# A decode block on one core: norm 2 folded around w_in, the weight loads reordered, and one V tile loaded in 112 + 8 + 8 rows

## The chip, the cores and the metric

The kernel runs on one core of one Trainium2 chip. The metric is the device time of one execution in microseconds (us); the times given are medians of repeated runs.

## The reference, cut to what matters

An adaptive-norm block for four tokens (B = 4, one position each): cached attention with 32 heads of 128 over 4096 keys, then a gated MLP ("gMLP"). The two caches, 4 x 32 x 4096 x 128 in bf16 each, are 268 MB of the 283 MB that are read.

```python
mod = (_silu(c) @ w_mod).reshape(c.shape[0], 6, 1, -1)
sa, ca, ga, sb, cb, gb = (mod[:, 0].copy(), ..., mod[:, 5].copy())
h = _layernorm(x, axis=-1) * (1 + ca) + sa
x = x + ga * _A_ref(h, A_k_cache, A_v_cache, A_wq, A_wo)
h = _layernorm(x, axis=-1) * (1 + cb) + sb
x = x + gb * _B_ref(h, B_w_in, B_w_sp, B_b_sp, B_w_out)
```

`_A_ref` is softmax attention of one query per head over the cache, then the product with `wo` (4096 x 512). `_B_ref` is `z = gelu(h @ w_in)` (512 x 1792), split in two halves of 896; the second half is layer-normed, scaled by `w_sp` and shifted by `b_sp` (one number each here, since there is one position), and multiplied with the first; then the product with `w_out` (896 x 512).

## The kernel before, in words

**Tiles.** The work on the caches is cut into 32 "quads" (`quads`, four heads of one token each): group g = 0 to 7 of heads outside, token b = 0 to 3 inside. For a quad, 4 heads x 4096 keys are laid on 128 partitions, 32 per head, so that each partition holds 128 keys of 128 elements: a K tile and a V tile of 128 x 16384 bf16 each, 4 MB, with one contiguous row of 32 KB per partition. `load` (L83) allocates a tile from two buffers and issues its loads on the SP queue. `load_v` (L95) and `load_k` (L92) load every tile with one DMA, except the last, which comes in column parts (V: a half, a quarter, two eighths), so that its work can begin with the first part.

**Order.** The program is scheduled by hand; each engine works its instructions in the order in which they stand. All loads that matter are on the SP queue[...]: `wm01` (the columns of w_mod for norm 1), `wq0`, K(0), K(1), wo of group 0, V(0), the rest of wq, and then in turn i: K(i+1), for b = 0 the tile `wo_g` of the group (512 KB, L368, read with 1 KB per partition and head), V(i). In turn 8 the columns 2 to 5 of w_mod follow (`wm25`, L382, 2 MB). After the last V come w_in (L409) and w_out (L411), into one tile.

**A turn i** of the loop at L362: `diagonal(i-2)`, the first half of `scores(i)` (DVE multiplies K with the query in place, L251; PE sums over the head dimension with the identity, L256), `project(i-2)`, the second half of the scores, `values(i-1)`, then `fold` and `softmax` of quad i. `values` (L299) multiplies the V tile with P on PE in four row groups (L309) and lets ACT drain the result (L315); ACT makes P with four Exp instructions (L286). `diagonal` (L322) picks the right block out of it. `zsum` (L295) gives the sum of P into one half of the PSUM tile `zo_ps`, whose other half takes the output. `project` takes the reciprocal (L344), scales (L345) and, for b = 3, adds the product with the group's wo to `attn_ps` (L352).

**The end.** The last quad takes another way: `values_last` (L333) multiplies block after block of V as weights with four columns of P, as the parts of V land, with filler matmuls (`keep_busy`, L127) between. Then x1 = x + ga * attn (L414, L415); the statistics of norm 2 (`ln_stats`, L147 to L165: square on DVE, one matmul with a constant, a reduction, Ln and Exp on ACT); the normed and modulated h2T (L420 to L424); 56 matmuls with w_in (L431); gelu (L438, L442); the statistics of norm 3; 28 matmuls with w_out (L449); the gate, scale and shift (L454 to L468); a transpose (L470) and the store. `mod_part` (L190) computes one of the six parts of `mod` with 16 matmuls; in turn 10 it is called for parts 2 to 5, with `wm25`.

Of the kernel before, what the change touches and what calls it, by code (L numbers as in the profile page):

```python
# [8 lines left out]
BF16 = mybir.dt.bfloat16  # L9
F32 = mybir.dt.float32  # L10
# [6 lines left out]
def kernel(  # L17
# [16 lines left out]
    nc = tc.nc  # L34
# [48 lines left out]
    def load(cache, i, tag, parts):  # L83
        t = kvp.tile([P, NT * DH], BF16, name=tag, bufs=2)
        a = 0
        for part in parts:
            b = a + NT * DH // part
            nc.sync.dma_start(out=t[:, a:b], in_=kv_view(cache, i)[:, a:b])
            a = b
        return t.rearrange("p (n d) -> p n d", d=DH)  # L90
# [2 lines left out]
        return load(A_k_cache, i, "kt", (2, 2) if i == len(quads) - 1 else (1,))  # L93

    def load_v(i):  # L95
        return load(A_v_cache, i, "vt", (2, 4, 8, 8) if i == len(quads) - 1 else (1,))

    NQ = len(quads)

# [22 lines left out]
    def keep_busy(n):  # L122

        if busy_ps[0] is None:
            busy_ps[0] = psum_s.tile([P, 4 * P], F32, name="big", bufs=2)
        for _ in range(n):
            nc.tensor.matmul(busy_ps[0], lhsT=ident, rhs=wide, start=True, stop=True)  # L127
# [14 lines left out]
    def bc(col, n):  # L142
        return col[:, None, :].to_broadcast([P, n, B])
# [24 lines left out]

    modT = persist.tile([P, 6, J, B], F32, name="modT")
    qbc = persist.tile([P, B, G, DH], BF16, name="qbc")  # L170
    x1b = persist.tile([P, 2, J, B], F32, name="x1b")
    wbf = persist.tile([P, 2], F32, name="wbf")
    xcT = persist.tile([P, J, 2 * B], F32, name="xcT")
# [8 lines left out]
        tc.tile_pool(name="psum_s", bufs=1, space=bass.MemoryType.PSUM)  # L182
    )

    def mod_part(wt, w0, oc):
        ps = psum_s.tile([P, J, B], F32, name="small", bufs=1)
        for jo in range(J):
            for j in range(J):
                c0 = (oc - w0) * D + jo * P
                nc.tensor.matmul(  # L190
                    ps[:, jo, :], lhsT=wt[:, j, c0:c0 + P],
                    rhs=sT[:, j, :], start=(j == 0), stop=(j == J - 1),
                )
        if oc in (1, 4):
            nc.vector.tensor_scalar_add(out=modT[:, oc], in0=ps, scalar1=1.0)
        else:
            nc.vector.tensor_copy(out=modT[:, oc], in_=ps)
# [46 lines left out]
    with tc.tile_pool(name="psum_att", bufs=1, space=bass.MemoryType.PSUM) as psum:  # L244
# [47 lines left out]
        def zsum(i):  # L292
            zo = psum.tile([P, 2, NH], F32, name="zo_ps", bufs=2)
            st["z", i], st["o", i] = zo[:, 0], zo[:, 1]
            nc.tensor.matmul(  # L295
                st["z", i], lhsT=ones_f, rhs=rs4s[i % NB], start=True, stop=True,
            )
# [29 lines left out]
        def values_last(i):  # L327
            P4 = P4s[i % NB]
            zsum(i)
            for n in range(NT):  # L330
                if n in (NT // 2, 3 * NT // 4, 7 * NT // 8):
                    keep_busy(2)
                nc.tensor.matmul(  # L333
                    st["o", i], lhsT=st["v", i][:, n, :], rhs=P4[:, n, :],
                    start=(n == 0), stop=(n == NT - 1),
                )

        def project(i):
            g, b = quads[i]
            if b == 0:  # L340
                st["oT", g] = wk.tile([P, NH, B], BF16, name="oT", bufs=2)
            oT = st["oT", g]
            rz = wk.tile([P, NH], F32, name="rz", bufs=2)
            nc.vector.reciprocal(out=rz, in_=st.pop(("z", i)))  # L344
            nc.vector.tensor_tensor(  # L345
                out=oT[:, :, b], in0=st.pop(("o", i)), in1=rz, op=ALU.mult,
            )
            if b == B - 1:
                wo_g = st.pop(("wo", g))
                for hl in range(NH):  # L350
                    for jo in range(J):
                        nc.tensor.matmul(  # L352
                            attn_ps[:, jo, :], lhsT=wo_g[:, hl, jo * P:(jo + 1) * P], rhs=oT[:, hl, :],
                            start=(g == 0 and hl == 0 and jo == 0),
                            stop=(g == G - 1 and hl == NH - 1),
                            skip_group_check=True,
                        )

        wo_v = A_wo.rearrange("(h p) n -> p h n", p=P)
        st["k", 0] = load_k(0)  # L360
        for i in range(NQ + 1):
            if i + 1 < NQ:  # L362
                st["k", i + 1] = load_k(i + 1)
            if i < NQ:
                if quads[i][1] == 0:
                    g = quads[i][0]
                    t = wk.tile([P, NH, D], BF16, name="wo_g", bufs=2)
                    nc.sync.dma_start(out=t, in_=wo_v[:, g * NH:(g + 1) * NH, :])  # L368
                    st["wo", g] = t
                st["v", i] = load_v(i)  # L370
                if i == 0:
                    wq_r = kvp.tile([P, J, (G - 1) * GW], BF16, name="wt", bufs=1)
                    nc.sync.dma_start(out=wq_r, in_=wq_v[:, :, GW:])
                if i in (2, 3):
                    for b in (2 * i - 4, 2 * i - 3):
                        for g0, n in ((1, 3), (4, 4)):
                            qp = psum_s.tile([P, n, DH], F32, name="big", bufs=2)
                            query(wq_r, 1, b, g0, n, qp, 0)
                            nc.scalar.copy(out=qbc[:, b, g0:g0 + n, :], in_=qp)  # L379
                if i == 8:  # L380
                    wm25 = kvp.tile([P, J, 4 * D], BF16, name="wt", bufs=1)
                    nc.sync.dma_start(out=wm25, in_=wmod_v[:, :, 2 * D:])  # L382
                if i == 10:
                    for oc in range(2, 6):
                        mod_part(wm25, 2, oc)
            if i > 1:
                diagonal(i - 2)
            if i < NQ:
                scores(i, 0)
            if i > 1:  # L390
                project(i - 2)
            if i < NQ:
                scores(i, 1)
            if 0 < i < NQ:
                values(i - 1)
            if i < NQ:
                fold(i, 0)
                fold(i, 1)
                softmax(i)
        keep_busy(3)  # L400
        values_last(NQ - 1)
        project(NQ - 1)
# [1 line left out]

    with tc.tile_pool(name="post", bufs=1) as post, \
            tc.tile_pool(name="psum_post", bufs=1, space=bass.MemoryType.PSUM) as psum:
        wt = kvp.tile([P, J * F + JF * D], BF16, name="wt", bufs=1)
        win = wt[:, 0:J * F].rearrange("p (j n) -> p j n", j=J)
        nc.sync.dma_start(out=win, in_=B_w_in.rearrange("(j p) n -> p j n", p=P))  # L409
        wout = wt[:, J * F:].rearrange("p (j n) -> p j n", j=JF)  # L410
        nc.sync.dma_start(out=wout, in_=B_w_out.rearrange("(p j) n -> p j n", j=JF))  # L411

        x1 = x1b[:, 0]
        nc.vector.tensor_tensor(out=x1, in0=attn_ps, in1=modT[:, 2], op=ALU.mult)  # L414
        nc.vector.tensor_tensor(out=x1, in0=x1, in1=xT, op=ALU.add)  # L415
        mean, rstd = ln_stats(post, psum_s, x1b, mean_d, J, "ln2")
        nc.scalar.preload_act_table_set("gelu_apprx_tanh_and_others")
        keep_busy(5)
        h2 = post.tile([P, J, B], F32, name="h2")
        nc.vector.tensor_tensor(out=h2, in0=x1, in1=bc(mean, J), op=ALU.subtract)  # L420
        nc.vector.tensor_tensor(out=h2, in0=h2, in1=bc(rstd, J), op=ALU.mult)
        nc.vector.tensor_tensor(out=h2, in0=h2, in1=modT[:, 4], op=ALU.mult)
        h2T = post.tile([P, J, B], BF16, name="h2T")
        nc.vector.tensor_tensor(out=h2T, in0=h2, in1=modT[:, 3], op=ALU.add)  # L424


        z_ps = psum.tile([P, 2, JF, B], F32, name="zf_ps")
        for s in (1, 0):
            for jf in range(JF):
                for j in range(J):  # L430
                    nc.tensor.matmul(  # L431
                        z_ps[:, s, jf, :], lhsT=win[:, j, s * FH + jf:(s + 1) * FH:JF],
                        rhs=h2T[:, j, :], start=(j == 0), stop=(j == J - 1),
                    )
        keep_busy(1)
        z2b = post.tile([P, 2, JF, B], F32, name="z2b")
        z2 = z2b[:, 0]
        nc.scalar.activation(out=z2, in_=z_ps[:, 1], func=AF.Gelu_apprx_tanh)  # L438


        u = post.tile([P, JF, 2, B], BF16, name="u")
        nc.scalar.activation(out=u[:, :, 1, :], in_=z_ps[:, 0], func=AF.Gelu_apprx_tanh)  # L442
        nc.scalar.preload_act_table_set("natural_log_exp_and_others")
        mean, rstd = ln_stats(post, psum_s, z2b, mean_f, JF, "ln3", lambda:
            nc.vector.tensor_tensor(out=u[:, :, 0, :], in0=u[:, :, 1, :], in1=z2, op=ALU.mult))
# [20 lines left out]
        )  # L466
        yo = post.tile([P, B, J], BF16, name="yo")
        nc.vector.tensor_tensor(out=yo.rearrange("p b j -> p j b"), in0=q, in1=r1, op=ALU.add)  # L468
        t_ps = psum.tile([J * B, P], F32, name="t_ps")
        nc.tensor.matmul(  # L470
            t_ps, lhsT=yo.rearrange("p b j -> p (b j)"), rhs=ident, start=True, stop=True,
        )
# [33 lines left out]
```

## Time and profile before

| | us |
|---|---|
| median of 10 runs (676.89 to 677.72) | 677.36 |
| the profiled execution | 677.3 |
| its span, first to last instruction | 675.4 |
| PE busy / DVE busy / ACT busy in the span | 419.6 / 375.8 / 102.9 |
| bytes read from HBM, mean rate | 282.73 MB, 419 GB/s |

The profile is one execution. "PEld" is the weight load of PE, which overlaps its matmuls. In the timeline a line gives start, duration, engine, line and operation, output and inputs with the shape, how many, and in brackets the idle time before and what ended it. DMA queues are named by number: q1 is that of SP, q8 and q14 carry instructions to the engines. The trace also has each DMA packet's start, duration and size, and for every DMA the times at which the DMA engines that take part report completion; it doesn't name the engine of a packet.

### The profile page before, as it was taken

The numbers are of one execution on the slowest core, as the hardware profiler recorded it, in microseconds if no ns is written. First come the engines' busy times: TensorE is split into PE (matmuls) and PEld (weight loads), VectorE is DVE, ScalarE is ACT, GpSimd is POOL, SyncE is SP. The second block draws the span as 40 slices with busy tenths as digits, with TensorE's granted clock in tenths as the row PEclk, the third lists the DMA queues.
The fourth block names the chain that finished last, engine by engine and source line by source line (L and its number), as shares of the span: only waits on it lengthen the run. The fifth ranks groups of instructions, "written<-read, shape, count | busy, mean of one in ns | idle before, by whom it ended". The sixth has DMA issues, their size and how long they took to land.

```text
span 675.4 us, 6968 instructions
## 1 busy us (share of the span) xinstructions
PE 419.6 (62%) x2979; PEld 205.5 (30%) x2983; DVE 375.8 (56%) x401; ACT 102.9 (15%) x311; POOL 4.1 (1%) x18
## 2 busy tenths in 40 slices
PE   2574857755657664567656457765555765565786
PEld 2232423322224222233223223332222322222344
DVE  2665555566653565545656455566654565664732
ACT  1021211101111011111011111101111101111112
POOL 2000000000000000000000000000000000000000
PEclk9977888766778676788667788766778876677885
DMA  9999999999999999999999999999999999999993
GB/s 373 414 423 434 430 434 422 428 429 432 435 428 416 433 430 433 426 431 428 431 428 427 432 435 422 426 431 433 430 429 420 434 433 433 432 419 432 426 413 127
DMA packets 16942, 283.17 MB, mean 419 GB/s; under 512 B 1416, under 2 KB 6032, under 8 KB 8464
## 3 DMA queue, kind: packets, MB, share of 16 engines
q1 hardware_dynamic: 16832, 282.73, 98.3%
q8 instruction: 23, 0.38, 0.2%
q14 instruction: 7, 0.06, 0.0%
q0 software_dynamic: 64, 0.00, 0.0%
q10 hardware_dynamic: 16, 0.01, 0.0%
HBM read 282.73 MB, written 0.00 MB: 419 GB/s over the span
## 4 chain that ended last, share of the span: by engine, by line
DMA 62%; PE 26%; DVE 10%; ACT 1%; issue 0%; SPq 0%; DVEq 0%; ACTq 0%
DMA kt<-in_A_k_cache_dram 57%; PE s_ps L256 22%; DVE kt L251 10%; DMA vt<-in_A_v_cache_dram 5%; PE big L309 1%; ACT P L286 1%; PE big L127 1%; PE zo_ps L333 0%; PE attn_ps L352 0%; PE zf_ps L431 0%; PE big L204 0%; PE zo_ps L322 0%; PE small L149 0%; PE zo_ps L295 0%; ACT osb L315 0%
## 5 line engine op out<-in xcount | busy, mean ns | idle before, releaser
L256 PE MATMUL s_ps<-kt,ident 128*128 128x512 bf16 x1024 | 294.1, 457 | 212.7 <-DVE kt L251 212.7
L251 DVE TENSOR_TENSOR kt<-kt,qbc 128x8192 bf16<-128x8192 bf16 x64 | 282.7, 4419 | 128.6 <-DMA kt<-in_A_k_cache_dram 128.6
L256 PEld LDWEIGHTS <-ident 128*128 128x128 bf16 x1024 | 115.6, 113 | 375.5 <-issue 225.4
L265 DVE TENSOR_REDUCE S<-s_ps 128x64 f32<-128x512 f32 x64 | 44.3, 692 | 128.8 <-PE s_ps L256 128.7
L315 ACT COPY osb<-big 128x512 f32<-128x512 f32 x31 | 18.2, 586 | 520.2 <-PE big L309 520.2
L286 ACT ACTIVATE P<-S,nm 32x128 bf16<-32x128 f32 x128 | 73.6, 575 | 21.1 <-DVE nm L283 18.8
L309 PE MATMUL big<-vt,P 128*32 128x512 bf16 x992 | 59.2, 380 | 0.4 <-DMA vt<-in_A_v_cache_dram 0.4
L322 PE MATMUL zo_ps<-sel,osb 128*128 128x4 f32 x248 | 34.2, 261 | 20.9 <-ACT osb L315 20.9
L322 PEld LDWEIGHTS zo_ps<-sel,osb 128*128 128x128 f32 x248 | 31.5, 199 | 36.0 <-ACT osb L315 34.7
L286 ACT ACTIVATION_READ_ACCUMULATOR P<-S,nm 32x1 f32 x128 | 31.8, 249 | 0.0
L309 PEld LDWEIGHTS <-P 128*32 128x32 bf16 x992 | 23.6, 96 | 21.3 <-DMA vt<-in_A_v_cache_dram 0.5
L295 PEld LDWEIGHTS zo_ps<-rs,ones_f 128*128 128x128 f32 x64 | 12.2, 192 | 5.6 <-ACT P L286 1.2
L344 DVE RECIPROCAL rz<-zo_ps 128x4 f32<-128x4 f32 x32 | 5.6, 176 | 10.3 <-PE zo_ps L333 7.4
L204 PE MATMUL big<-wt,hbc 128*32 128x384 bf16 (+1 forms) x128 | 8.1, 396 | 3.8 <-ACT qbc L379 3.6
L273 DVE TENSOR_REDUCE mx<-S 128x1 f32<-128x128 f32 x32 | 9.2, 286 | 1.3
L295 PE MATMUL zo_ps<-rs,ones_f 128*128 128x4 f32 x64 | 9.2, 214 | 0.7 <-ACT P L286 0.7
L204 PEld LDWEIGHTS <-hbc 128*32 128x32 bf16 x192 | 5.5, 112 | 10.7 <-issue 6.6
L283 DVE STREAM_TRANSPOSE nm<-hb 128x32 f32<-128x32 f32 x32 | 6.8, 212 | 3.2
L275 DVE STREAM_TRANSPOSE mT<-mx 128x32 f32<-128x32 f32 x32 | 6.8, 212 | 1.1
L277 DVE TENSOR_REDUCE hm<-mT 128x1 f32<-128x32 f32 x32 | 6.0, 186 | 1.1
L279 DVE TENSOR_SCALAR hb<-hm 128x32 f32<-128x32 f32 x32 | 5.8, 181 | 1.1
L345 DVE TENSOR_TENSOR oT<-zo_ps,rz 128x4 bf16<-128x4 f32 x32 | 5.4, 168 | 1.1
(88 smaller groups left out, 71.0 us busy)
## 6 DMA issues: line engine op xcount, KB each, us to landing
kt<-in_A_k_cache_dram SPq DMA_DIRECT2D x31, 4096.0 KB, 25.7
vt<-in_A_v_cache_dram SPq DMA_DIRECT2D x31, 4096.0 KB, 34.4
wo_g<-in_A_wo_dram SPq DMA_DIRECT2D x8, 512.0 KB, 26.5
kt<-in_A_k_cache_dram SPq DMA_DIRECT2D x2, 2048.0 KB, 24.3
wt<-in_A_wq_dram SPq DMA_DIRECT2D x1, 3584.0 KB
wt<-in_w_mod_dram SPq DMA_DIRECT2D x1, 2048.0 KB, 38.4
vt<-in_A_v_cache_dram SPq DMA_DIRECT2D x1, 2048.0 KB, 19.3
wt<-in_B_w_in_dram SPq DMA_DIRECT2D x1, 1792.0 KB
```

Of the source, the lines that this page charges most:

```text
L204: nc.tensor.matmul(qp[hl * R:(hl + 1) * R, col:col + n], lhsT=hbc[:, j, b, :], rhs=wv[:, g0 - hl0:g0 - hl0 + n, hl, :], start=(j == 0), st ...
L251: nc.vector.tensor_tensor(out=kt, in0=kt, in1=q[:, None, :].to_broadcast([P, HT, DH]), op=ALU.mult,)
L256: nc.tensor.matmul(ps, lhsT=ident, rhs=kt[:, :, cc * DC:(cc + 1) * DC], start=(cc == 0), stop=(cc == DH // DC - 1),)
L265: nc.vector.tensor_reduce(out=st["S", i][:, half * HT:(half + 1) * HT], in_=st.pop(("s", i, half)), axis=AX.X, op=ALU.add,)
L273: nc.vector.tensor_reduce(out=mx[:, 0:1], in_=S, axis=AX.X, op=ALU.max)
L275: nc.vector.transpose(out=mT, in_=mx)
L283: nc.vector.transpose(out=nm, in_=hb)
L286: nc.scalar.activation(out=P4[rows, 0:NT, hl], in_=S[rows, :], func=AF.Exp, bias=nm[rows, 0:1], scale=att_scale, accum_out=rs4[rows, hl:hl ...
L295: nc.tensor.matmul(st["z", i], lhsT=ones_f, rhs=rs4s[i % NB], start=True, stop=True,)
L309: nc.tensor.matmul(po[32 * t:32 * t + 32], lhsT=P4[:, n0:n0 + 8, :], rhs=st["v", i][:, n0:n0 + 4, :], start=(u == 0), stop=(u == NU - 1), ...
L315: nc.scalar.copy(out=osb, in_=po)
L322: nc.tensor.matmul(st["o", i], lhsT=osb[:, n, :], rhs=sel[:, NH * n:NH * n + NH], start=(n == 0), stop=(n == 3),)
```

## The change

**Norm 2 folded.** With h = (x1 - mean) * rstd * (1 + cb) + sb, the product with w_in is rstd * ((x1 * (1 + cb)) @ w_in - mean * ((1 + cb) @ w_in)) + sb @ w_in. The new tile `hx` holds the three right-hand sides, twelve columns: x1 * (1 + cb), (1 + cb) and sb. `z_half(s)` multiplies one half of w_in with them; the first half stands ahead of the statistics of norm 2 on PE, the second behind; `z_norm(s)` combines the three results in four DVE steps. The fillers there go.

**Loads.** In turn 8 only the columns of parts 2 to 4 of w_mod are loaded (1.5 MB); those of part 5 (the gate gb) come behind w_in, which is loaded in two halves, and ahead of w_out. `wo_g` is read, except in the last group, with four consecutive rows of wo per partition (4 KB contiguous); as its rows are then in another order, 16 small matmuls with every fourth column of the identity put the attention output of the group into the same order (`apply`, which moves from `project` to the end of the turn).

**The last V tile** comes in five parts instead of four, with the fillers spread accordingly, and its sum of P has a PSUM tile of its own.

**V(4)** is loaded with three DMAs: partitions 0 to 111, 112 to 119, 120 to 127.

```diff
     def load_v(i):
-        return load(A_v_cache, i, "vt", (2, 4, 8, 8) if i == len(quads) - 1 else (1,))
+        if i == 4:
+
+            t = kvp.tile([P, NT * DH], BF16, name="vt", bufs=2)
+            for a, b in ((0, 112), (112, 120), (120, 128)):
+                nc.sync.dma_start(out=t[a:b], in_=kv_view(A_v_cache, i)[a:b])
+            return t.rearrange("p (n d) -> p n d", d=DH)
+        return load(A_v_cache, i, "vt", (2, 4, 8, 16, 16) if i == len(quads) - 1 else (1,))
...
+    hx = persist.tile([P, J, 3, B], BF16, name="hx")
...
-    def mod_part(wt, w0, oc):
-        ps = psum_s.tile([P, J, B], F32, name="small", bufs=1)
+    def mod_part(wt, w0, oc, ps=None):
+        if ps is None:
+            ps = psum_s.tile([P, J, B], F32, name="small", bufs=1)
...
             st["z", i], st["o", i] = zo[:, 0], zo[:, 1]
+            if i == NQ - 1:
+                st["z", i] = psum_s.tile([P, NH], F32, name="small", bufs=1)
...
-                if n in (NT // 2, 3 * NT // 4, 7 * NT // 8):
-                    keep_busy(2)
+                if n in (NT // 2, 3 * NT // 4, 7 * NT // 8, 15 * NT // 16):
+                    keep_busy(2 if n < 7 * NT // 8 else 1)
...
+            if i == NQ - 1:
+                apply(i)
+
+        def apply(i):
+            g, b = quads[i]
             if b == B - 1:
+                oT = st.pop(("oT", g))
                 wo_g = st.pop(("wo", g))
+                if g < G - 1:
+
+                    pp = psum_s.tile([P, NH, B], F32, name="small", bufs=1)
+                    for r in range(NH):
+                        for hl in range(NH):
+                            nc.tensor.matmul(
+                                pp[hl * R:(hl + 1) * R, r, :], lhsT=ident[:, r::NH],
+                                rhs=oT[:, hl, :], start=True, stop=True,
+                                tile_position=(0, hl * R),
+                            )
+                    oT = wk.tile([P, NH, B], BF16, name="oP", bufs=2)
+                    nc.vector.tensor_copy(out=oT, in_=pp)
                 for hl in range(NH):
...
-        wo_v = A_wo.rearrange("(h p) n -> p h n", p=P)
+
+        wo_w = A_wo.rearrange("(g p r) n -> g p r n", p=P, r=NH)
+        wo_v = A_wo.rearrange("(g h p) n -> g p h n", h=NH, p=P)
...
-                    nc.sync.dma_start(out=t, in_=wo_v[:, g * NH:(g + 1) * NH, :])
+                    nc.sync.dma_start(out=t, in_=(wo_v if g == G - 1 else wo_w)[g])
...
-                    wm25 = kvp.tile([P, J, 4 * D], BF16, name="wt", bufs=1)
-                    nc.sync.dma_start(out=wm25, in_=wmod_v[:, :, 2 * D:])
+                    wm24 = kvp.tile([P, J, 3 * D], BF16, name="wt", bufs=1)
+                    nc.sync.dma_start(out=wm24, in_=wmod_v[:, :, 2 * D:5 * D])
                 if i == 10:
-                    for oc in range(2, 6):
-                        mod_part(wm25, 2, oc)
+                    for oc in range(2, 5):
+                        mod_part(wm24, 2, oc)
+                    nc.vector.tensor_copy(out=hx[:, :, 1, :], in_=modT[:, 4])
+                    nc.vector.tensor_copy(out=hx[:, :, 2, :], in_=modT[:, 3])
...
+            if 1 < i < NQ:
+                apply(i - 2)
...
-        wt = kvp.tile([P, J * F + JF * D], BF16, name="wt", bufs=1)
+        wt = kvp.tile([P, J * F + JF * D + J * D], BF16, name="wt", bufs=1)
         win = wt[:, 0:J * F].rearrange("p (j n) -> p j n", j=J)
-        nc.sync.dma_start(out=win, in_=B_w_in.rearrange("(j p) n -> p j n", p=P))
-        wout = wt[:, J * F:].rearrange("p (j n) -> p j n", j=JF)
+        win_v = B_w_in.rearrange("(j p) n -> p j n", p=P)
+        for s in (1, 0):
+            nc.sync.dma_start(
+                out=win[:, :, s * FH:(s + 1) * FH], in_=win_v[:, :, s * FH:(s + 1) * FH],
+            )
+        wm5 = wt[:, J * F + JF * D:].rearrange("p (j n) -> p j n", j=J)
+        nc.sync.dma_start(out=wm5, in_=wmod_v[:, :, 5 * D:])
+        wout = wt[:, J * F:J * F + JF * D].rearrange("p (j n) -> p j n", j=JF)
         nc.sync.dma_start(out=wout, in_=B_w_out.rearrange("(p j) n -> p j n", j=JF))
...
-        mean, rstd = ln_stats(post, psum_s, x1b, mean_d, J, "ln2")
-        nc.scalar.preload_act_table_set("gelu_apprx_tanh_and_others")
-        keep_busy(5)
-        h2 = post.tile([P, J, B], F32, name="h2")
...
+        nc.vector.tensor_tensor(out=hx[:, :, 0, :], in0=x1, in1=hx[:, :, 1, :], op=ALU.mult)
+        zp = {}
+
+        def z_half(s):
+            zp[s] = psum.tile([P, JF, 3, B], F32, name=f"z{s}_ps")
             for jf in range(JF):
                 for j in range(J):
                     nc.tensor.matmul(
-                        z_ps[:, s, jf, :], lhsT=win[:, j, s * FH + jf:(s + 1) * FH:JF],
-                        rhs=h2T[:, j, :], start=(j == 0), stop=(j == J - 1),
+                        zp[s][:, jf], lhsT=win[:, j, s * FH + jf:(s + 1) * FH:JF],
+                        rhs=hx[:, j], start=(j == 0), stop=(j == J - 1),
                     )
-        keep_busy(1)
+
+        def z_norm(s):
+            t = post.tile([P, JF, B], F32, name=f"zn{s}")
+            nc.vector.tensor_tensor(out=t, in0=zp[s][:, :, 1, :], in1=bc(mean, JF), op=ALU.mult)
+            nc.vector.tensor_tensor(out=t, in0=zp[s][:, :, 0, :], in1=t, op=ALU.subtract)
+            nc.vector.tensor_tensor(out=t, in0=t, in1=bc(rstd, JF), op=ALU.mult)
+            nc.vector.tensor_tensor(out=t, in0=t, in1=zp[s][:, :, 2, :], op=ALU.add)
+            return t
+
+
+        z_half(1)
+        mean, rstd = ln_stats(post, psum_s, x1b, mean_d, J, "ln2")
+        nc.scalar.preload_act_table_set("gelu_apprx_tanh_and_others")
+        z_half(0)
+        mod_part(wm5, 5, 5, psum.tile([P, J, B], F32, name="m5_ps"))
         z2b = post.tile([P, 2, JF, B], F32, name="z2b")
         z2 = z2b[:, 0]
-        nc.scalar.activation(out=z2, in_=z_ps[:, 1], func=AF.Gelu_apprx_tanh)
+        nc.scalar.activation(out=z2, in_=z_norm(1), func=AF.Gelu_apprx_tanh)
...
-        nc.scalar.activation(out=u[:, :, 1, :], in_=z_ps[:, 0], func=AF.Gelu_apprx_tanh)
+        nc.scalar.activation(out=u[:, :, 1, :], in_=z_norm(0), func=AF.Gelu_apprx_tanh)
...
-        t_ps = psum.tile([J * B, P], F32, name="t_ps")
+        t_ps = psum_s.tile([J * B, P], F32, name="small", bufs=1)
```

More of the change, by code (lines that the diff above doesn't have):

```diff
@@ L415 @@
         nc.vector.tensor_tensor(out=x1, in0=x1, in1=xT, op=ALU.add)
-        mean, rstd = ln_stats(post, psum_s, x1b, mean_d, J, "ln2")
-        nc.scalar.preload_act_table_set("gelu_apprx_tanh_and_others")
-        keep_busy(5)
-        h2 = post.tile([P, J, B], F32, name="h2")
[L420 to L428, printed above, removed]
+        nc.vector.tensor_tensor(out=hx[:, :, 0, :], in0=x1, in1=hx[:, :, 1, :], op=ALU.mult)
+        zp = {}
+        def z_half(s):
+            zp[s] = psum.tile([P, JF, 3, B], F32, name=f"z{s}_ps")
             for jf in range(JF):
```

## The prediction, made blind

> **What bounds the kernel now.** I read the page's slices and queues first. `DMA` is the mean busy share of the 16 DMA engines, `GB/s` what they moved:
>
> ```profile
> DMA  9999999999999999999999999999999999999993
> GB/s 373 414 423 434 430 434 422 428 429 432 435 428 416 433 430 433 426 431 428 431 428 427 432 435 422 426 431 433 430 429 420 434 433 433 432 419 432 426 413 127
> ...
> q1 hardware_dynamic: 16832, 282.73, 98.3%
> q8 instruction: 23, 0.38, 0.2%
> ```
>
> The engines are full from the first slice to the last but one: every microsecond of transfer ahead of the last tiles is a microsecond of the kernel, and PE, DVE and ACT have slack before that. Then the timeline of the last 30 us (start, duration, engine, line):
>
> ```profile
> 650.14 1.91 PE L309 MATMUL big<-vt,P 128*32 128x512 bf16 x32 [0.40 <-DMA vt<-in_A_v_cache_dram]
> 652.15 0.59 ACT L315 COPY osb<-big 128x512 f32<-128x512 f32 x1 [13.40 <-PE big L309]
> ...
> 655.18 0.51 PE L295 MATMUL zo_ps<-rs,ones_f 128*128 128x4 f32 x2 [0.67 <-ACT P L286]
> ...
> 661.05 0.61 PE L333 MATMUL zo_ps<-P,vt 128*128 128x4 bf16 x16
> ...
> 661.70 0.18 DVE L344 RECIPROCAL rz<-zo_ps 128x4 f32<-128x4 f32 x1 [7.43 <-PE zo_ps L333]
> ...
> 665.98 3.12 PE L431 MATMUL zf_ps<-h2T,wt 128*128 128x4 bf16 x56
> ...
> 669.61 0.68 PE L149 MATMUL small<-z2b,mean_f 128*128 128x56 f32 x2 [0.51 <-DVE z2b L147]
> ```
>
> Values of quad 30 wait for its V tile, which lands at 650.09; ACT drains them, then makes the last P, and from 655.18 PE runs the last values, with the fillers of L127 between, until 661.66, almost without a pause. The last V part lands at 660.08, over 1 us before its matmuls start at 661.25, so the set point is the landing of V(30); everything after follows it at fixed distance.
>
> Third, the completion events of the trace, one per DMA engine and DMA. V(30) completes on its engines between 644.98 and 650.09: offsets 0, 0.10, 0.30, 0.35, 0.52, 0.82, 2.06, 2.89, 3.18, 3.41, 3.63, 4.71, 4.73, 4.81, 4.82, 5.11. Early on the spread was 0.5. The engines drift apart because 16 KB instruction packets (queue q8, 21 of them before 655) sit between the data packets; each sets one engine back about 1.5 us (the first at 18.02: the spread goes from 0.48 to 1.98). Their durations repeat with period eight, so the same eight engines take them in turn: five have 3, three have 2. **The slowest engine, not the mean, ends a tile.** The other eight carry at most 2.89. The 4-row load of x at 4.76 can be followed by packet times into the first K tile: its four engines stand there at 0, 0.01, 0.01 and 0.06, the earliest, while the engine of the first instruction packet stands at 0.43.
>
> [...] a 32 KB packet follows the last after 1.212 us, 27.0 GB/s per engine; [...] packets of 1024 B take 43 to 46 ns each, 4096 B about 160, against 37.9 ns per KB in 32 KB packets. [...]
>
> **The change part by part**, against the profiled execution (677.3 us, span 675.4, so 1.9 around it; the median of the runs is 677.36).
>
> *wm25 to wm24.* 32 packets per engine of 4096 B become 3072 B. Its landing comes 5.08 after the V ahead (204.91 to 209.99). A line through 32768 B (1212 ns) and 4096 B (157) gives 6.3 ns + 0.0368 per B: 119 ns at 3072 B, 3.84 for 32. **-1.24 us**, on the path.
>
> *wo with four rows per partition.* 7 of 8 loads go from 32 packets of 1 KB to 8 of 4 KB per engine. Such a load takes 1.41 to 1.49 now (515.65 to 517.12 for instance), 8 x 0.160 + 0.01 = 1.29 after: 7 x 0.17 = **-1.2**. The price is 16 small matmuls (35 ns each in L352) and a DVE copy (0.2) per group, about 1 us in 7 of 32 turns; PE and DVE wait for K in each turn (128.6 us of DVE idle before L251), so 0; without that cover 7. apply stands at the end of a turn; queued behind it on PE is the next diagonal, on DVE the next K product, which wait for DMA anyway. [...] one more q8 packet before V(30), on an engine that has 2; it goes from 3.2-3.6 to about 5 and passes nobody: 0, at worst 0.1.
>
> *The tail*, from the end of the last values matmul E. Before: reciprocal and oT to 0.46, L352 to 1.06, x1 to 1.47, statistics to 3.5, Ln and Exp, four DVE steps to 4.2, 56 matmuls to 7.46, gelu, statistics of norm 3 at 7.95. After: the last z has its own tile, so the reciprocal is done early (-0.22); x1 to 1.27, product with 1+cb 1.48, z_half(1) (28 x 56 ns) 1.6 to 3.2, statistics 3.85, rstd 5.05, z_half(0) 5.4, sixteen matmuls of wm5 6.0, their copy on DVE 6.2. z_norm(1) stands behind that copy on DVE: four steps to 7.0; gelu 7.2; z_norm(0) to 7.7; square 7.9; norm 3 at 7.96. **0**: what folding hides, eight steps on DVE and the copy give back. -1.0 if these pair better or the clock (0.5 here) is granted, +1.0 if wm5 is late. By packet sizes wm5 lands 2 x 2.31 (1792 B) + 1.47 = 6.1 after the last V, that is E + 4.5, needed at 5.4; w_out at E + 6.7, needed at 8.6: cover 0.9 and 1.9. Split of the last V in five, keep_busy of 1 for 2, fewer of them, two more issues on SP (0.33 each, 20 us ahead of use): 0; PE still has six fillers in the values chain. On SP the issue of w_out lasts 9.97 us already (638.89)[...]; w_in's halves, wm5 and w_out will be held likewise, behind nothing but each other and out, with some 60 packets still ahead of them on the slowest engine.
>
> Sum so far: **-2.45**.
>
> *V(4) as 112 + 8 + 8 rows.* No trace row has this. [...] **Lower bound:** ports don't matter. Lower engines +1.21, upper -1.21: V(30) then ends at max(2.89+1.21, 5.11-1.21) = 4.10 for 5.11: -1.0. **Upper bound:** [...] A row of 32 KB then takes 4 to 5 x 1.205 = 4.8 to 6.0. Engines 0 to 7: 7 x 1.21 + 2 x (4.8 to 6.0) = 18.1 to 20.5 for 9.7 before: +8.4 to +10.8, which nothing undoes later[...]. With their 2.89 they end at 11.3 to 13.7 for 5.11: +6.2 to +8.6. [...] some tenths more. **I take +7.8**[...]. 16 us are queued ahead of a K at its issue (574.83 to 599.98 less its own 9.7), so the lag starves no slow engine.
>
> Sum: 677.3 - 2.45 + 7.8 = 682.65, **682.7 us**.
>
> **The rivals.** *Ports carry more than one engine's rate* (the other side): place, the sixteen last rows of V(4); price -1.0 for +7.8[...]. [...] 677.3 - 3.45 = **673.8**. *Part of the contention*[...]: +3 to +5, **679.5**. *The drifting engines are the lower ones, or eight rows spread evenly*, ports harmless: +1.2 or 0 on -2.45, **676.1** or 674.9. Against the first: the engines followed from x.
>
> **Numbers.** Contention 0.48 (own range 680.8 to 685.0), part of it 0.10 (0.03 of that within 0.2%), ports harmless 0.33, the last pair 0.09 (0.07 within 0.2%). 0.2%, about what a measurement of this kernel can tell from no change, is 676.0 to 678.7. Faster 0.33 + 0.02 = 0.35, same 0.10, slower 0.48 + 0.07 = 0.55. The range has to reach both sides: 673.0 to 685.0, the ends of the contention case and of the harmless one with 0.8 of the tail's doubt.
>
> **What would show it.** wo landings 1.3 behind the V ahead; wm24 3.85; at V(4) completions of eight engines 8 us or more behind, kept to the end, and 32 KB packets of 5 to 6 us near 120 to 140 us. If all packets there stay at 1.2 us, the spread at V(30) falls to about 4.1 and the harmless case holds. In the tail: the sixteen matmuls of wm5 ending 6 us after E, the statistics of norm 3 starting at about 8. A PE wait for wm5, or a last V landing after its matmuls could start, would break the tail's zero.

## The result, and the profile after

| kernel | median us | runs | ratio to before, 95% interval |
|---|---|---|---|
| before | 677.29 | 28 | |
| after | 691.0 | 8 | 1.0204 [1.0195, 1.0213] |

The change makes the kernel 13.7 us slower. The profiled execution has a span of 689.2 us, 13.8 more than before. Forecast were 682.7 us and a range up to 685.0: the sign was the likeliest one, the size lies outside.

First the slices and queues of the page, for the kernel after:

```profile
DMA  9999999989999999999999999999999999999993
GB/s 366 425 426 433 435 429 373 192 364 440 428 426 424 433 427 434 431 428 429 436 427 430 431 433 432 431 430 429 430 431 434 425 433 432 427 424 431 436 394 119
...
q1 hardware_dynamic: 15360, 282.73, 98.2%
q8 instruction: 24, 0.39, 0.2%
```

The two rows have to be read against each other. `DMA` is as full as before, but `GB/s` has a hole in the seventh to ninth slice: 373, 192 and 364 where some 430 are moved elsewhere. The bytes are the same (282.73 MB); the packets are fewer, above all by the 4 KB rows of wo. Finer, from the table by stretches (us, busy us of each engine, TensorE clock, DMA share, GB/s), after:

```profile
100.00:116.00 16.00, 12.58 (x74) 5.70 (x73) 8.47 (x11) 2.83 (x9) 0.00 (x0) 0.80 1.02 421
116.00:130.00 14.00, 8.43 (x27) 3.35 (x28) 9.70 (x5) 0.06 (x2) 0.00 (x0) 0.63 1.03 248
130.00:142.00 12.00, 1.44 (x9) 0.77 (x6) 1.77 (x6) 0.00 (x0) 0.00 (x0) 0.66 0.97 153
142.00:156.00 14.00, 5.97 (x72) 4.06 (x73) 4.40 (x2) 2.90 (x9) 0.00 (x0) 0.50 0.99 425
```

and the same stretches before:

```profile
116.00:130.00 14.00, 8.98 (x44) 3.84 (x45) 9.71 (x5) 0.00 (x0) 0.00 (x0) 0.63 0.99 424
130.00:142.00 12.00, 4.17 (x48) 2.61 (x47) 6.33 (x9) 2.89 (x9) 0.00 (x0) 0.77 1.01 433
```

Over 26 us the engines are "busy" for 1.03 and 0.97 of the time and move 248 and 153 GB/s. So a packet counts as busy for as long as it lasts. These are the microseconds in which V(4) and the first rows of the K tile behind it, K(6), are written. By the packet records the 32 KB packets that start from 117 to 128 last 2.18 us in the median (1.22 before), and from 120 on sixteen of them are in flight at once, so all engines are slow; from 128 on come, among shorter ones, packets of 3.2 to 5.25 us. Summed over the packets and divided by sixteen, the excess over 1.215 us, about the time of such a packet before, is 14.1 us an engine between 112 and 160: 6.6 in packets of up to 3 us, 7.5 in the longer ones. K(6) lands at 151.76 for 137.39.

The end, from the timeline of the kernel after (start, duration, engine, line):

```profile
662.67 3.40 PE L320 MATMUL big<-vt,P 128*32 128x512 bf16 x32 [1.91 <-DMA vt<-in_A_v_cache_dram]
...
666.16 0.59 ACT L326 COPY osb<-big 128x512 f32<-128x512 f32 x1 [16.40 <-PE big L320]
...
669.18 0.39 PE L306 MATMUL small<-rs,ones_f 128*128 128x4 f32 x2 [0.66 <-ACT P L295]
...
669.61 0.18 DVE L355 RECIPROCAL rz<-small 128x4 f32<-128x4 f32 x1 [1.33 <-PE small L306]
...
675.12 0.40 PE L344 MATMUL zo_ps<-P,vt 128*128 128x4 bf16 x8
...
677.40 1.63 PE L467 MATMUL z_ps<-hx,wt 128*128 128x12 bf16 x28 [1.06 <-DMA wt<-in_B_w_in_dram]
...
680.79 0.57 PE L199 MATMUL m_ps<-sT,wt 128*128 128x4 bf16 x16
...
683.39 0.64 PE L155 MATMUL small<-z2b,mean_f 128*128 128x56 f32 x2 [2.04 <-DVE z2b L153]
```

V(30) lands at 662.62, 12.5 later than before, and PE waits for it as before. The same 32 matmuls then take 3.40 us instead of 1.91, +1.5: the granted clock of TensorE was 0.54 in that stretch and 1.00 before. What lies between them and the end of the last values matmul (called E from here on; 675.52 here, 661.66 before) is 0.2 shorter, and from E to the end of the copy into ot, the output tile, 11.10 pass, 11.21 before, -0.1. With 12.5 that makes the 13.8.

### The profile page after: what moved, and what is told of

Its sections match the earlier page's. It is cut to its first block, busy times and chain, and to the rows that moved or that the text cites. A ratio compares the mean times of both kernels' runs of the same rounds, so it can differ in the third digit from the quotient of the medians.

```text
span 689.2 us, 7204 instructions
## 1 busy us (share of the span) xinstructions
PE 420.4 (61%) x3086; PEld 207.8 (30%) x3089; DVE 378.0 (55%) x415; ACT 103.1 (15%) x311; POOL 4.1 (1%) x18
## 3 DMA queue, kind: packets, MB, share of 16 engines
q1 hardware_dynamic: 15360, 282.73, 98.2%
HBM read 282.73 MB, written 0.00 MB: 410 GB/s over the span
## 4 chain that ended last, share of the span: by engine, by line
DMA 66%; PE 22%; DVE 11%; issue 0%; SPq 0%; DVEq 0%
DMA kt<-in_A_k_cache_dram 62%; PE s_ps L265 21%; DVE kt L260 10%; DMA wt<-in_B_w_in_dram 4%; PE z_ps L467 0%; PE small L155 0%; PE y_ps L499 0%; DVE S L274 0%; SPq L75 0%; PE m_ps L199 0%; SPq L71 0%; DVE zn L476 0%; DVE zn L475 0%; DVE zn L477 0%; SPq L88 0%
## 5 line engine op out<-in xcount | busy, mean ns | idle before, releaser
L320 PE MATMUL big<-vt,P 128*32 128x512 bf16 x992 | 62.4, 395 | 12.9 <-DMA vt<-in_A_v_cache_dram 12.9
L320 PEld LDWEIGHTS <-P 128*32 128x32 bf16 x992 | 24.5, 99 | 35.4 <-issue 13.8
```

The source lines that it names most:

```text
L320: nc.tensor.matmul(po[32 * t:32 * t + 32], lhsT=P4[:, n0:n0 + 8, :], rhs=st["v", i][:, n0:n0 + 4, :], start=(u == 0), stop=(u == NU - 1), ...
```

## The experiments

In all but two of these kernels the work and the bytes are those of the reference; the two load some bytes more, which their expectations say. The landings and packets are those of one profiled execution of each kernel, the times medians of all.

"Ports theory" names the author's assumption that the time depends on which partitions the engines write to at the same moment; no trace shows a port. "Engines 0 to 7" are in these texts the eight that take the loads of eight rows: in the trace after, each of these two loads of V(4) has eight completion events, the one of 112 rows sixteen. The numbers, and that the same eight take both, are the author's; the trace gives none.

### The change without V(4), and V(4) alone

```diff
-        if i == 4:
...
-            for a, b in ((0, 112), (112, 120), (120, 128)):
-                nc.sync.dma_start(out=t[a:b], in_=kv_view(A_v_cache, i)[a:b])
```

Taken out of the kernel after:

> The changed kernel with V(4) in one DMA of 128 rows again. Ports theory (the whole loss comes from V(4)[...]): 674.9 us, that is 2.4 below before, V(30) landing 2.4 earlier. Rival (folding norm 2, the new order of loads and wo's new layout cost something themselves): above 677. The first is right if it is under 676.

Put into the kernel before:

> The kernel before with V(4) in 112 + 8 + 8 rows and nothing else. Ports theory: 677.3 + 13.7 + 2.4 = 693 us, packets of V(4) at about 2.2 us and those of the eight-row loads at 4 to 5 us. Row-count rival (only nine rows for seven on half of the engines matters, the rest of the loss is from the other edits): 676 to 679.

Two more put another split of V(4) into the kernel before: (0, 64), (64, 128), and (0, 112), (112, 128).

> The kernel before with V(4) in two DMAs of 64 rows[...]. Ports theory: [...] 9.7 us of transfer become 19.4, 687 us, packets at 2.4 us. Row-count rival: 677.3, packets at 1.21 us.

> The kernel before with V(4) in 112 + 16 rows[...]. Ports theory: seven packets of 2.2 us and one of 4.8[...] for eight of 1.21, +10.5, 688 us. Row-count rival: 677.3.

| kernel | median us (runs) | ratio to before | V(30) lands | excess of 32 KB packets, us per engine |
|---|---|---|---|---|
| without V(4) | 675.21 (9) | 0.9974 [0.9964, 0.9984] | 647.03 | none |
| V(4) alone | 691.65 (4) | 1.0225 [1.0209, 1.0241] | 664.47 | 12.8 |
| 64 + 64 | 689.37 (4) | 1.0181 [1.0167, 1.0195] | 662.04 | 11.9 |
| 112 + 16 | 689.53 (4) | 1.0184 [1.0170, 1.0198] | 662.56 | 12.3 |

Before, V(30) lands at 650.09. The whole loss lies in how V(4) is cut; the rest of the change is a small gain. The ports theory's times are missed by 0.3 us in the first kernel and by 1.4 to 2.4 in the other three; the row-count rival's by 12 or more. 64 + 64 was meant to leave every engine as many rows as another, so that only the place of the rows differs; still the packets take about twice their time, 2.54 us in the median for 1.21. The stretches of that kernel:

```profile
116.00:130.00 14.00, 9.01 (x50) 4.20 (x50) 9.78 (x6) 0.19 (x2) 0.00 (x0) 0.76 0.96 196
130.00:142.00 12.00, 2.14 (x24) 0.95 (x28) 1.69 (x6) 0.00 (x0) 0.00 (x0) 0.67 0.98 262
```

196 GB/s is a little under half of the 424 before.

### Neighbouring partitions, and partitions four apart

The last eighth of the columns of V(4) is cut off and loaded by sixteen DMAs of 8 rows, in the one kernel of neighbouring partitions, in the other of partitions that lie four apart (of the two lines for `s`, each kernel has one).

```diff
+            kv, c = kv_view(A_v_cache, i), 7 * NT * DH // 8
+            nc.sync.dma_start(out=t[:, :c], in_=kv[:, :c])
+            for r in range(16):
+                s = slice(8 * r, 8 * r + 8)       # neighbouring
+                s = slice(32 * (r // 4) + r % 4, 32 * (r // 4) + 32, 4)   # four apart
+                nc.sync.dma_start(out=t[s, c:], in_=kv[s, c:])
```

> The kernel before, with the last eighth of the columns of V(4) cut off its 128-row load and loaded by sixteen DMAs of 8 neighbouring partitions (4 KB packets[...]). Nothing is left out. If neighbouring partitions share a port: 16 packets an engine at 4 x 0.157 us instead of 0.157 make 7.2 us; 684.5 us if the whole machine waits, about 682 if only engines 0 to 7 lose and their lead of 3 us or so takes part of it. In the trace the packets of engines 8 to 15[...] tell these two apart: near 1.21 us each, or 2 us and more. If the number of rows were what costs, or nothing: about 676.3, as the bytes moved from engines 8 to 15 to engines 0 to 7 are worth 1.0 us.

> As the run with neighbouring partitions, the same bytes by the same engines in the same sixteen DMAs, but each DMA takes 8 partitions that lie 4 apart[...]. Nothing is left out. Ports theory: no packet much over its own time, 0.157 us for 4 KB; V(30) lands 1.0 us earlier by the moved bytes and the time is 676.3 us, at worst 677.5 where engines 0 to 7 turn out not to lead. If it is small DMAs, or fewer rows than 128, that cost: 682 us or more, as with neighbouring partitions.

Measured: 682.6 us (4 runs; 1.0086 [1.0071, 1.0102]) and 684.5 us (4 runs; 1.0110 [1.0096, 1.0124]). The second one misses its expectation by 8 us, and the two times tell nothing about the place of the rows, since the queues ran dry. The issues on SP of the kernel with rows four apart, from its timeline:

```profile
92.58 0.33 SPq L99 DMA_DIRECT2D vt<-in_A_v_cache_dram  x1
92.96 39.27 SPq L102 DMA_DIRECT2D vt<-in_A_v_cache_dram  x16
132.35 0.37 SPq L88 DMA_DIRECT2D kt<-in_A_k_cache_dram  x1
```

The sixteen issues lasted 39.27 us, and the trace shows what they went with: the fourth to the eighth each went out within 0.02 us of the landing of the DMA issued eight before it. The eighth, at 126.26, followed the 128-row part of V(4) itself, landed at 126.24. From then on they went out one every 0.66 us (0.33 with neighbouring partitions), as one issue of rows four apart took 0.62 us, one of neighbouring rows 0.29. The next K, which goes out at about 111 in the kernel before, was issued only after them, at 132.35. Its stretches:

```profile
124.00:128.00 4.00, 4.00 (x29) 1.80 (x28) 2.06 (x2) 0.00 (x0) 0.00 (x0) 0.73 0.26 101
128.00:134.00 6.00, 4.79 (x48) 2.26 (x46) 1.77 (x6) 0.00 (x0) 0.00 (x0) 1.00 0.45 128
```

A DMA share of 0.26 and 0.45 is the opposite picture to that of the kernel after, where it stays near 1: here the engines have nothing to do, there each packet takes longer.

The first seven of the sixteen DMAs went out while the loads ahead of them were still in flight, and their packets do tell the two kernels apart. With rows four apart all 56 packets of 4 KB take 0.159 to 0.164 us; with neighbouring rows they take 0.234 in the median and up to 0.44. Packets of 28 KB that start beside them, from 123 to 128, last at most 1.07 us in the first kernel and up to 1.78 in the second. To show it in the time as well, a few large DMAs are needed.

### The same rows to partitions four apart or to neighbouring ones

Four extra DMAs of 8 rows each go into a spare tile, behind V(5) of the kernel before. Sources, sizes and number are the same in both kernels; only the partitions differ (of the two lines for `out`, each kernel has one).

```diff
+                if i == 5:
+                    w = 7 * NT * DH // 8
+                    spare = kvp.tile([P, w], BF16, name="wt", bufs=1)
+                    for r in range(4):
+                        nc.sync.dma_start(
+                            out=spare[slice(r, 32, 4), :],             # four apart
+                            out=spare[slice(8 * r, 8 * r + 8), :],     # neighbouring
+                            in_=kv_view(A_v_cache, i)[8 * r:8 * r + 8, :w],
+                        )
```

> The kernel before plus four extra DMAs behind V(5): each reads 8 neighbouring rows of V(5) (28 KB of each row) into a spare tile[...]. Here row j of DMA r goes to partition r + 4j[...]. Nothing of the computation is changed; 0.9 MB more is loaded. Ports theory: packets of 28,672 B take 1.06 us each, engines 0 to 7 lose 4 x 1.06 = 4.25 us, of which their lead at V(30) (2.89 against 5.11) takes 2.2; V(30) lands 2.0 later, 679.3 us; if the lead is not theirs, 681.5. Source theory (eight neighbouring rows of HBM read at once, or an 8-row DMA as such, is what is slow): packets of 3 to 5 us and 690 us or more, as in the run that differs only in where the rows go.

> The same four extra DMAs with the same sources, sizes and engines as the run with own ports; only where the rows go differs: row j of DMA r goes to partition 8r + j[...]. Nothing of the computation is changed; 0.9 MB more is loaded. Ports theory: a packet takes 4 x 1.06 = 4.25 us, four of them 17 us on engines 0 to 7; the others[...], lose nearly as much if a waiting write holds up everything (packets of 3 us and more on their 128-row loads meanwhile); V(30) lands 14 to 17 us later, 691 to 694 us. If only engines that share a port lost, engines 8 to 15 would keep 1.21 us a packet; the end would still be near 692. Source theory: the same as the run with own ports, within 0.5 us.

Four apart ("own ports" in the texts): 680.28 us (4 runs; 1.0046 [1.0032, 1.0059]), V(30) at 652.43, +2.3, and its time lies between the two that the ports theory allowed. All 32 extra packets take 1.062 to 1.069 us and no other packet near them is long. Neighbouring: 690.55 us (4 runs; 1.0187 [1.0168, 1.0207]), just under the range expected; V(30) at 665.84 in the profiled execution, the slowest of the four (693.12). The 32 extra packets take 3.23 to 4.08 us. One stretch of each, first four apart, then neighbouring:

```profile
144.00:162.00 18.00, 9.36 (x69) 4.82 (x68) 6.31 (x9) 2.90 (x9) 0.00 (x0) 0.78 0.98 422
```

```profile
144.00:162.00 18.00, 10.09 (x69) 4.81 (x67) 4.69 (x8) 2.91 (x9) 0.00 (x0) 0.78 1.01 138
```

Same source rows, same DMA sizes, a DMA share of 0.98 and 1.01, and 422 against 138 GB/s. Neither the 8-row DMA nor eight neighbouring rows of HBM is the cause; where the rows go is. And the ordinary 128-row loads, which the other eight engines write beside them, also take 3.3 to 5.1 us for most of their 32 KB packets (1.21 before). So while eight engines write to neighbouring partitions, the others are held up too.

### The end of the kernel

The kernel without V(4) gains 0.26%, 1.8 us by the ratio, where the steps of the prediction sum to 2.45. Its timeline:

```profile
647.72 0.28 PE L300 MATMUL zo_ps<-rs,ones_f 128*128 128x4 f32 x2
...
647.93 1.91 PE L314 MATMUL big<-vt,P 128*32 128x512 bf16 x32
...
661.85 1.63 PE L461 MATMUL z_ps<-hx,wt 128*128 128x12 bf16 x28 [1.75 <-DMA wt<-in_B_w_in_dram]
```

V(30) has landed at 647.03, 3.06 earlier than before, but the values of L314 show no wait for it: PE comes out of the scores of quad 31 only at 647.7. E is 2.38 earlier. Then the first folded product waits 1.75 us for w_in, until both halves are there (659.48 and 661.76), although it reads only the first. Two edits on that kernel: the halves in two contiguous ranges of the tile, and, in addition, the copy of the wm5 product behind the product u.

```diff
-        win = wt[:, 0:J * F].rearrange("p (j n) -> p j n", j=J)
...
+            win[s] = wt[:, (1 - s) * J * FH:(2 - s) * J * FH].rearrange("p (j n) -> p j n", j=J)
...
-                out=win[:, :, s * FH:(s + 1) * FH], in_=win_v[:, :, s * FH:(s + 1) * FH],
+            nc.sync.dma_start(out=win[s], in_=win_v[:, :, s * FH:(s + 1) * FH])
...
-                        zp[s][:, jf], lhsT=win[:, j, s * FH + jf:(s + 1) * FH:JF],
+                        zp[s][:, jf], lhsT=win[s][:, j, jf:FH:JF],
```

> The change without its V(4) part, with the two halves of w_in in two contiguous ranges of the tile (before, each half was a strided range between the other's pieces). Nothing is left out. Theory: the first half of the folded product waits for the second half of w_in only because the two ranges overlap as intervals; it will start 1.0 us earlier (near E+1.55 instead of E+2.57), gelu with it until the activation table and the copy of the last gate columns (wm5) limit it: 674.3 us, 0.9 under the kernel without this edit (675.2). Rival: the wait is for something else (the two loads share a counter, or hx), and the start stays at E+2.57: 675.2.

```diff
+        def between():
+            nc.vector.tensor_tensor(out=u[:, :, 0, :], in0=u[:, :, 1, :], in1=z2, op=ALU.mult)
+            nc.vector.tensor_copy(out=modT[:, 5], in_=m5_ps)
```

> As the run with w_in in two ranges, and the copy of the wm5 product out of PSUM moved on VectorE from ahead of the normalization of z to behind the product u. Nothing is left out. Theory: z's normalization no longer waits for wm5 (landing E+3.85, product and copy E+6.5), and the activation table's load sets gelu: 0.3 us less, 674.0 us. Rival: the table's load sets it in both, no difference (674.3).

Measured: 673.55 us (5 runs; 0.9950 [0.9937, 0.9962]) and 673.05 us (5 runs; 0.9940 [0.9928, 0.9953]). With the halves apart:

```profile
660.15 1.63 PE L460 MATMUL z_ps<-hx,wt 128*128 128x12 bf16 x28 [0.77 <-DVE x1b L147]
...
664.14 0.17 DVE L200 COPY modT<-m_ps 128x16 f32<-128x16 f32 x1 [1.27 <-PE m_ps L193]
664.23 0.18 DVE L467 TENSOR_TENSOR zn<-z_ps,st_ln 128x28 f32<-128x28 f32 x1
```

The product starts at E + 1.60 instead of E + 2.57, and its wait is now for DVE. The normalization of z (L467) starts right behind the copy of L200. With the copy deferred:

```profile
662.71 0.18 DVE L469 TENSOR_TENSOR zn<-z_ps,st_ln 128x28 f32<-128x28 f32 x1
...
663.37 1.28 ACT L478 ACT_TABLE_LOAD   x1
...
664.67 0.23 ACT L484 ACTIVATE z2b<-zn 128x28 f32<-128x28 f32 x1
```

The same step, now L469, starts 1.5 us earlier, and gelu (L484) follows the table load of ACT, the next limit. The second kernel's gain over the first, 0.5 us, lies within their intervals; over the kernel before each is a gain beyond its interval, and both are some 2.5% faster than the kernel after. The version of 673.05 us is the best one here.

### The change without V(4) and without the new wo

> The change without its V(4) part and with wo as before (1 KB packets, no permutation matmuls). Nothing is left out. By the prediction's step, seven wo loads cost 0.17 us each: V(30) lands 1.2 us later than with four rows per partition. As the scores of quad 31 on TensorE end only 0.9 us after V(30) lands there, part of the 1.2 is hidden: 675.8 us, 0.6 above the run with the new wo (675.2). Rivals: the whole 1.2 shows (676.4), or nothing does, because TensorE sets the end (675.2).

```diff
-                    nc.sync.dma_start(out=t, in_=(wo_v if g == G - 1 else wo_w)[g])
+                    nc.sync.dma_start(out=t, in_=wo_v[g])
...
-                if g < G - 1:
...
```

Measured: 676.86 us (13 runs; 0.9995 [0.9987, 1.0003]), no difference from before. It is 1.65 above the kernel with the new wo, 1.4 by the two ratios to before. The rival that the whole worth of wo shows holds, and it is more than the 1.2 forecast. V(30) lands at 648.57, 1.54 later than with the new wo (the seven loads save 0.22 each) and 1.52 earlier than before. What the smaller wm24 brings is given back at the end:

```profile
663.63 1.63 PE L448 MATMUL z_ps<-hx,wt 128*128 128x12 bf16 x28 [3.23 <-DMA wt<-in_B_w_in_dram]
```

Here the wait for both halves of w_in is 3.23 us, the product starts at E + 4.05. That also says why nothing of wo is hidden: the second half of w_in, the last load that the product waits for, lands at 663.54 here and at 661.76 with the new wo, and the profiled executions end 1.8 apart. In these two kernels the end follows the queue of loads, not E.

## Why the prediction was wrong

**The failing step is the term for V(4)**: "some tenths more" for the blocks of seven rows, and the charge of the eight-row loads to one half of the engines alone. That the time depends on which partitions are written together holds (422 against 138 GB/s for the same rows four apart and neighbouring), so the sign was right for a good reason. But the step rested on an assumption about how the engines reach the partitions, which no run shows, and charged only the engines that write to the same place by it. All sixteen lose: the first of K(6)'s sixteen completion events comes 12.8 later than before, the last 14.4.
- The 112 rows, put at some tenths, cost about 6.6 us an engine (the packets of up to 3 us): 2.18 us a packet in place of 1.21. Why all sixteen engines run near half rate there is not shown.
- The 8-row loads and what runs beside them, put at 2 x (4.8 to 6.0) on eight engines, cost about 7.5 an engine, on all sixteen; the longer packets there took 3.2 to 5.25. The factor of 4 to 5 in that price was an assumption; these packets took 2.6 to 4.3 times their 1.21.
- The lead of 2.2 us of the early engines, which the step took off, was therefore not to be had: the slowest ones lost as much.

So +7.8 was +14.2 in the kernel after: K(6) ends 13.8 later in the mean of its engines, with 0.43 saved by two loads of wo ahead of it. That "nothing undoes" the delay later was right: 14.2 less 3.06 is 11.1, and K(31), the last K, lands 11.0 later.

**A line read wrongly, without effect**: the last eighth of V is used from 661.05 on, as the line shown has it, not from 661.25, so it landed 0.97 ahead and not over 1 us.

**wm24**: 3.84 forecast, 3.86 to 3.88 measured. Right.

**wo**: 1.29 a load forecast, 1.24 to 1.27 measured; -1.2 became -1.54. Right, a little small. The cover of the permutation held.

**One more instruction packet "passes nobody"**: wrong in the kernel after, though true without V(4). That one packet more would come was the author's estimate; queue q8 has 24 for 23. Between K(31) and V(30) the offset of the slowest engine goes from 5.62 to 7.17, and no other offset moves by more than 0.1; one instruction packet, at 659.36, lies between them, so it fell on just that engine: +1.5. In the kernel without V(4) the extra packet comes at 646.20 and the spread stays at 4.94. With 11.0 that gives the 12.5 of V(30).

**"Everything after follows it at fixed distance" (V(30))**: true while the delay lasts, false for gains. Without V(4) the landing gained 3.06 and E only 2.38, as the scores of quad 31 on PE became the later one.

**The tail at 0**: -0.1 after, but +0.6 without V(4) and, measured to the copy into ot, +2.1 with the old wo. Its first step, z_half(1) at E + 1.6, failed: E + 1.88, 2.57 and 4.05 in these three, since it waits for both halves of w_in. With the halves apart it starts at E + 1.60. That norm 3 still came at E + 7.87 for 7.96 in the kernel after is luck: the start was only 0.28 late there; without V(4) it was 0.97 late, and norm 3 came at E + 8.56. The doubt had been laid on wm5, and that was never waited for.

**The rivals.** "Ports carry more than one engine's rate" put V(4) at -1.0 and "part of the contention" at +3 to +5, for 14.2 measured in the kernel after and 11.9 to 12.8 with V(4) alone in its three splits. A sign for the first was seen in the four packets of x, 1 KB each at 46 ns, as long as other packets of 1 KB; it misled: they told nothing of 32 KB ones.

## What to carry to other kernels

A large load of 128 rows is best left in one DMA over the 128 partitions until a run shows another split to be as fast: the three tried here on V(4), 112 + 8 + 8, 112 + 16 and 64 + 64, cost 1.8 to 2.3% of the kernel each, and where small loads are needed, their partitions matter (1.06 us a packet four apart, 3.23 to 4.08 neighbouring). Where the DMA share stays full and GB/s falls (0.97 and 153 here), look at packet durations; where both fall (0.26 and 101), look at the issuing queue. And when a load is cut so that work can start on its first part, try separate contiguous ranges of the tile for the parts (here the start went from E + 2.57 to E + 1.60), and a gain of a microsecond at the last load has to be followed to the next engine that is late.

## What was not expected of the hardware

- Packets without any of the extra rows are held as well: in the run with neighbouring partitions the ordinary loads beside them took mostly 3.3 to 5.1 us a packet for 1.21. What lets the slow writes hold the others is left open; no run here separates it.
- In the kernel with sixteen small DMAs of rows four apart, five issues on SP, the fourth to the eighth, each went out within 0.02 us of the landing of the DMA eight before it, and the sixteen lasted 39.27 us. And one issue of 8 rows four apart took 0.62 us for 0.29 of neighbouring ones.
- The granted clock at one moment, 0.54 for 1.00, made the same 32 matmuls take 3.40 us for 1.91, a tenth of the loss in the profiled execution. With V(4) alone they take 1.91; no run here shows how often it happens.
